# GpSimd takes over the splitting of queries and keys for four head pairs, and ScalarE scales one left-over probability tile

## The chip, the cores and the metric

The kernel runs on one core of one Trainium2 chip. The metric is the time of one execution on the device in microseconds; lower is better. The kernel before was timed three times.

## The reference, cut to what matters

Three stages follow each other, all in fp32, for 4 batches of 576 tokens with 8 heads of 64 (512 columns):

```python
# 1 attention with a threshold under the row's maximum
scores = scale * q @ k.T
scores = where(scores >= max(scores) - tau, scores, -1e9)
attn = exp(scores - max) / (sum + 1e-9)
x = attn @ v
# 2 a mixture over the sequence, then a channel MLP (512 -> 2048 -> 512)
u = x + (x.T @ U @ V).T
x = u + relu(u @ w_ch1) @ w_ch2
# 3 one of eight experts per token (512 -> 1024 -> 512), chosen by a gate
out = p[e] * (relu(x @ w1[e]) @ w2[e])
```

## The kernel before, in words

**Precision.** Most products are made from a high and a low part: the high part is the operand rounded to fp32r, the low part is the operand less the high part. For keys the scores multiply the queries with `kh` and with `kl`. For queries the 128 rows of `qs` hold the 64 rows of high parts above the 64 rows of low parts. Splitting a piece of raw data therefore takes a rounding copy and a subtraction.

**Pairs.** The heads are worked on two at a time, so a batch has four pairs; pair `i = 4 b + hp` belongs to batch `b`. `load_pair` (line 256 on) brings a pair in and splits it. Four pieces of a pair go through a ring of three buffers called `raw`: keys of 576 columns, keys of 640, queries of 608, queries of 608. In pairs 1 to 15, ScalarE makes the key's high part (L292) and the scaled query's rounded copy (L300), and VectorE makes the query's low half (L302). The key's low part (L293) is made by GpSimd in batches 0 and 1, and by VectorE later. In pair 0 two query pieces of 448 and 256 columns are already split by three GpSimd instructions each (L296 multiply in place, L297 rounding copy, L298 subtraction on 64 rows).

**Batch 0.** `attention_alone(0)` runs the attention of the first batch with no other matrix work beside it. A pair has five groups of rows, and nine score tiles of 128 rows by 576 keys: two tiles in groups 0 to 3 and one in group 4, which holds the left-over 64 rows of both heads. Per tile TensorE makes the scores (L321, L323), VectorE finds the row maximum (`peak`, L356) and the limits (L360), ScalarE the exponential (`exp`, L367) and VectorE the mask with the row sums (`mask`, L371). TensorE then transposes the masked tile (L427, and L433 to L438 for group 4), ScalarE moves it out of PSUM (L428, L434 to L440), and TensorE multiplies by V. Two score tiles fit in PSUM. The load of the next pair begins at its pair's third tile, one piece per tile.

**Normalization.** In batches 1 to 3 ScalarE multiplies every tile by the reciprocal row sums before the transposes (L381, in `norm`). In batch 0 the division is done late, in `chain`, once the product with V has been turned back into rows. For the left-over group that needs the second head's reciprocal on other partitions, which a small transfer on SP's queue brings there (L384), and two ScalarE instructions of 64 columns with two scales (L486).

**Beside batch 0.** `narrow` brings the 64-bit channel weights in as raw bits (`cr`, a ring of three), ScalarE casts one half (`top`, L212) and VectorE joins the halves (`w`, L219); the result is written to `wdram` and read back by `load_w` (`wr`), which splits it. In batch 0's channel weights ScalarE makes the high parts for `f` 0 and 1 (L692) and GpSimd for the other fourteen (L690); GpSimd makes the low parts (L693).

**Later.** From batch 1 on, `interleave` mixes the attention of one batch with the channel MLP of the batch before. The experts come last.

**Order.** A planner lays down each engine's order at compile time from its own estimates and the order of the program. GpSimd keeps the order of the program in batch 0's attention. Each engine, and SP's DMA queue too, then works strictly in the order laid down; a waiting instruction holds all that is behind it.

Of the kernel before, what the change touches and what calls it, by code (L numbers as in the profile page):

```python
# [14 lines left out]
AF = mybir.ActivationFunctionType  # L15
# [11 lines left out]
NPAIR = H // 2  # L27
# [76 lines left out]
def attention_channel_moe(ctx, tc, qk, vv, tau, umat, vrep, wch, wgl, wexp, consts, out):  # L104
# [156 lines left out]
    def load_pair(b, hp, later=None):  # L261

        i = b * NPAIR + hp
        v = ap.tile([128, VW], F32, tag="v", name=f"v{i}")
        qs = ap.tile([128, QKW], F32R, tag="qs", name=f"qs{i}")
        kh = ap.tile([128, QKW], F32R, tag="kh", name=f"kh{i}")
        kl = ap.tile([128, QKW], F32R, tag="kl", name=f"kl{i}")

        cuts = ((1, 0, S), (0, 0, 128), (1, S, QKW), (0, 704, 832), (0, 128, 256), (0, 832, 960),
                (0, 256, 704), (0, 960, QKW)) if i == 0 else (  # L270
            (1, 0, S), (1, S, QKW), (0, 0, 608), (0, 608, QKW))
        eng = dve if i == 0 or b > 1 else pool
        def steps():
            for n, (kq, c0, c1) in enumerate(cuts):
                c = slice(c0, c1)
                nm = f"raw{i}_{n}"
                if (i, n) == (0, 0):
                    x = mlp.tile([128, S], F32, tag="yr", name=nm, bufs=2)
                elif i == 0 and c1 - c0 == 128:
                    x = mlp.tile([128, 512], F32, tag="wr", name=nm, bufs=WR)  # L280
                else:
                    x = ap.tile([128, 640], F32, tag="raw", name=nm, bufs=3)
                x = x[:, :c1 - c0]
                sp.dma_start(out=x, in_=qk[i][:, kq, c])
                if (i, n) == (0, 1):
                    scalars()
                if (i, n) == (0, 5):
                    sp.dma_start(out=cst, in_=consts)
                if (i, n) == (0, 7):
                    sp.dma_start(out=wg_sb, in_=wgl)  # L290
                if kq:
                    act.activation(kh[:, c], x, AF.Copy)  # L292
                    eng.tensor_tensor(out=kl[:, c], in0=x, in1=kh[:, c].bitcast(F32), op=ALU.subtract)  # L293
                elif i == 0 and c1 - c0 > 128:
                    lo, hi, xl = qs[64:128, c], qs[64:128, c].bitcast(F32), x[64:128]
                    pool.tensor_scalar(out=x, in0=x, scalar1=t8[:, 1:2], scalar2=None, op0=ALU.mult)  # L296
                    pool.tensor_copy(qs[:, c], x)  # L297
                    pool.tensor_tensor(out=lo, in0=xl, in1=hi, op=ALU.subtract)  # L298
                else:
                    act.activation(qs[:, c], x, AF.Copy, scale=t8[:, 1:2])  # L300
                    lo, hi, xl = qs[64:128, c], qs[64:128, c].bitcast(F32), x[64:128]
                    dve.scalar_tensor_tensor(out=lo, in0=xl, scalar=t8[64:128, 1:2], in1=hi,  # L302
                                             op0=ALU.mult, op1=ALU.subtract)
                yield
            sp.dma_start(out=v, in_=vv[i])

        if later is None:
            for _ in steps():
                pass
        else:  # L310
            later.append(steps())
        return qs, kh, kl, v
# [13 lines left out]
    class Group:  # L326
# [47 lines left out]
        def norm(self):  # L374

            g = self.key[2]
            rv = self.rvs[:, g, 0:self.nh]
            if self.b >= SCALED:
                inverse(rv)
                for h in range(self.nh):  # L380
                    act.activation(self.pt[:, h], self.pt[:, h], AF.Copy, scale=rv[:, h:h + 1])  # L381
            elif g == 4:
                inverse(rv)
                sp.dma_start(out=self.rvs[:64, 4, 1:2], in_=self.rvs[64:, 4, 0:1])  # L384

    def inverse(x, on_act=False):
        if on_act:
# [70 lines left out]
    def chain(nm, hp, half, xT, xu, rvs):  # L458

        o, n = HALVES[half]  # L460
        if half == 0:
            if XS[0] is None:
                XS[0] = ap.tile([128, 5, 128], F32, tag="xsd", name=f"xsd{nm}", bufs=1)
                dve.memset(XS[0][64:, 4], 0.0)
        xsd = XS[0]
        c0, c1 = ((0, 2), (2, 5))[half]
        if rvs is not None:
            inverse(rvs[:, c0:c0 + 2], on_act=True)
        tp = po_tile(f"tx{nm}").rearrange("p (a b) -> p a b", a=4)
        for c in range(c0, c1):  # L470
            w = 64 if c == 4 else 128
            pe.transpose(tp[:w, c - c0], xu[:, c * 128 - o:c * 128 - o + w], ident)
        if rvs is None:
            dve.tensor_copy(xsd[:, c0:c0 + 2], tp[:, :2])
        else:
            dve.tensor_tensor(out=xsd[:, c0:c0 + 2].rearrange("p c (h d) -> p c h d", h=2),
                              in0=tp[:, :2].rearrange("p c (h d) -> p c h d", h=2),
                              in1=rvs[:, c0:c0 + 2].unsqueeze(3).to_broadcast([128, 2, 2, 64]), op=ALU.mult)
        if half == 0:
            yield 0.3  # L480
            return
        if rvs is None:
            act.activation(xsd[:64, 4], tp[:64, 2], AF.Copy)
        else:
            for h in range(2):
                act.activation(xsd[:64, 4, h * 64:h * 64 + 64], tp[:64, 2, h * 64:h * 64 + 64], AF.Copy,  # L486
                               scale=rvs[:64, 4, h:h + 1])
        yield 0.3
        while not MIXED[0]:
            next(conv)  # L490
        pst = po_tile(f"tT{nm}")[:, :128]

        for r, c in zip((0, 32, 64, 96), (4, 2, 3, 0)):
            pe.matmul(pst[r:r + 32], lhsT=u_sb[:, c], rhs=xsd[:, c], start=True, stop=False)
        for r in (0, 32, 64, 96):
            pe.matmul(pst[r:r + 32, r:r + 32], lhsT=u_sb[:, 1], rhs=xsd[:, 1, r:r + 32], start=False, stop=True)
        tT = ap.tile([128, 128], F32, tag="tT", name=f"tT{nm}", bufs=1)
        act.activation(tT, pst, AF.Copy)
        yield 0.7

        pr = po_tile(f"rep{nm}")[:, :128]
        pe.matmul(pr, lhsT=cst[:, C_REP:C_REP + 128], rhs=tT, start=True, stop=True)
        th = ap.tile([128, 128], F32R, tag="th", name=f"th{nm}", bufs=1)
        act.activation(th, pr, AF.Copy)
        dve.tensor_tensor(out=th[64:], in0=pr[64:], in1=th[64:].bitcast(F32), op=ALU.subtract)
        yield 0.3
        for (o, n), (c0, c1) in zip(HALVES, ((0, 2), (2, 5))):
            pu = po_tile(f"pu{nm}_{o}")
            u = xT[:, hp, o:o + n]
            if rvs is None:  # L510
                pe.matmul(pu[:, :n], lhsT=th, rhs=vst[:, o:o + n], start=True, stop=True)
                dve.tensor_tensor(out=u, in0=pu[:, :n], in1=u, op=ALU.add)
                yield 0.2
                continue
            for c in range(c0, c1):
                q = c * 128 - o
                pe.matmul(pu[:, q:q + 128], lhsT=xsd[:, c], rhs=ident, is_transpose=True, start=(c == c0), stop=False)
            pe.matmul(pu[:, :n], lhsT=th, rhs=vst[:, o:o + n], start=False, stop=True)
            act.activation(u, pu[:, :n], AF.Copy)  # L519
            yield 0.45  # L520
# [155 lines left out]
    def load_w(b, f):  # L676
        nm = f"{b}_{f}"
        if f >= NF or nm in W:
            return
        while DONE[0] < f:  # L680
            next(conv, None)
        r = []
        for i, bufs in ((0, W0), (1, W1)):
            x = mlp.tile([128, 512], F32, tag="wr", name=f"wr{nm}_{i}", bufs=WR)
            sp.dma_start(out=x, in_=wdram[f * 128:f * 128 + 128, i * 512:i * 512 + 512])
            hi = mlp.tile([128, 512], F32R, tag=f"w{i}h", name=f"w{i}h{nm}", bufs=bufs)
            lo = mlp.tile([128, 512], F32R, tag=f"w{i}l", name=f"w{i}l{nm}", bufs=bufs)
            eng = dve if b and (b < B - 1 or f < 8) else pool
            if b == 0 and f > 1:
                pool.tensor_copy(hi, x)  # L690
            else:
                act.activation(hi, x, AF.Copy)  # L692
            x = eng.tensor_tensor(out=lo, in0=x, in1=hi.bitcast(F32), op=ALU.subtract)  # L693
            if i == 0:
                LAST[:] = [x.ins]
            r.append((hi, lo))
        W[nm] = r
# [693 lines left out]
```

## Time and profile before

| | |
|---|---|
| time, median of 3 runs | 1032.04 us (1027.95 to 1032.97) |
| the profiled execution's own time | 1023.09 us |
| its span from first to last instruction | 1021.3 us |
| TensorE busy | 991.2 us (97%) |
| VectorE busy | 714.6 us (70%) |
| ScalarE busy | 612.4 us (60%) |
| GpSimd busy | 157.3 us (15%) |
| mean granted TensorE clock | 0.995 |

The busy times are sums over the whole span; the stages differ. TensorE's busy time counts matmuls that overlap in its pipeline.

### The profile page before, as it was taken

The page shows a single profiled execution, that of the slowest core. Times are in us where ns is not written, and L with a number is a line of the kernel's source. Part 1 is how long each engine was busy: PE and PEld are TensorE (multiplying, and loading weights), DVE is VectorE, ACT ScalarE, POOL GpSimd, SP SyncE. Part 2 cuts the span into 40 slices and gives each one's busy share as a digit, 9 for nine tenths or more (in the row PEclk, how much of TensorE's full clock was granted, in tenths as well). Part 3 has the DMA queues.
Part 4 walks back from the last instruction along what each step waited for, and adds up shares of the span by engine and source line. Part 5 has one row for each costly group of instructions (what it writes and reads, how often), then busy time and mean ns, then how long its engine had stood idle before and what let it go on. Part 6 is the DMA issues. An engine that isn't in the chain of part 4 may idle for free. (4 is left out here: it accounts for less than half of the span.)

```text
span 1021.3 us, 17791 instructions
## 1 busy us (share of the span) xinstructions
PE 991.2 (97%) x6308; PEld 830.7 (81%) x6309; DVE 714.6 (70%) x1764; ACT 612.4 (60%) x1250; POOL 157.3 (15%) x149
## 2 busy tenths in 40 slices
PE   8898999999999999999999999999999999999996
PEld 4666677778777787788888898999998898889884
DVE  7888686786778877777676564692369855566673
ACT  6898777776587776776575653422344444355562
POOL 3332246342000000000000000014400321020100
PEclk9999999999999999999999999999999999999998
DMA  6755487863322322322121110454054655566550
GB/s 212 240 149 174 155 271 229 282 206 127 125 93 95 115 87 71 125 98 87 56 69 42 42 44 30 140 201 137 27 199 167 209 175 186 174 197 202 187 185 17
DMA packets 58529, 143.72 MB, mean 141 GB/s; under 512 B 7421, under 2 KB 8573, under 8 KB 58432
## 3 DMA queue, kind: packets, MB, share of 16 engines
q1 hardware_dynamic: 55072, 132.27, 39.5%
q0 software_dynamic: 3360, 10.23, 3.1%
q8 instruction: 52, 0.85, 0.3%
q14 instruction: 45, 0.37, 0.1%
HBM read 124.65 MB, written 18.61 MB: 140 GB/s over the span
## 5 line engine op out<-in xcount | busy, mean ns | idle before, releaser
L1141 ACT ACTIVATE eh<-ew 128x512 fp32r<-128x512 f32 x160 | 94.2, 628 | 68.5 <-PE el L1257 54.0
L1142 DVE TENSOR_TENSOR el<-ew,eh 128x512 fp32r<-128x512 f32 x160 | 106.8, 692 | 38.6 <-ACT eh L1141 37.1
L714 PE MATMUL l<-uh,w0h 128*128 128x256 f32 (+2 forms) x352 | 126.8, 361 | 0.3 <-ACT yT L519 0.3
L371 DVE SCALAR_TENSOR_TENSOR p<-s,st,p 128x576 f32<-128x576 f32 x144 | 114.1, 815 | 18.3 <-ACT p L367 14.6
L367 ACT ACTIVATE p<-s,st 128x576 f32<-128x576 f32 x144 | 103.5, 738 | 34.2 <-DVE st L356 33.0
L715 PE MATMUL l<-ul,w0h 128*128 128x256 f32 (+2 forms) x352 | 122.6, 348 | 0.0
L716 PE MATMUL l<-uh,w0l 128*128 128x256 f32 (+2 forms) x352 | 122.3, 348 | 0.0
L356 DVE TENSOR_REDUCE st<-s 128x1 f32<-128x576 f32 x144 | 105.3, 750 | 16.4 <-PE s L323 15.4
L729 PE MATMUL l<-hh,w1h 128*128 128x512 f32 (+3 forms) x320 | 115.3, 360 | 0.0
L731 PE MATMUL l<-hh,w1l 128*128 128x512 f32 (+3 forms) x320 | 112.6, 352 | 0.0
L730 PE MATMUL l<-hl,w1h 128*128 128x512 f32 (+3 forms) x320 | 112.2, 351 | 0.0
L428 ACT ACTIVATE ptt<-tp 128x512 f32<-128x512 f32 (+1 forms) x192 | 88.5, 489 | 29.5 <-PE tp L427 29.2
L693 POOL TENSOR_TENSOR w1l<-wr,w1h 128x512 fp32r<-128x512 f32 x24 | 31.9, 1337 | 453.8 <-DVE rha L999 426.1
L321 PE MATMUL s<-kh,qs 128*128 128x288 f32 x320 | 95.8, 319 | 5.0 <-DVE p L371 2.7
L427 PE MATMUL tp<-cst,p 128*128 128x128 f32 x576 | 91.6, 276 | 3.9 <-ACT ptt L428 3.6
L734 DVE TENSOR_TENSOR yT<-l,yT 128x448 f32<-128x448 f32 (+2 forms) x96 | 50.0, 521 | 57.7 <-PE l L731 57.2
L323 PE MATMUL s<-kl,qs 128*128 128x288 f32 x320 | 88.9, 297 | 0.0
L381 ACT ACTIVATE p<-p,rv 128x576 f32<-128x576 f32 x108 | 78.6, 771 | 16.6 <-DVE rv L391 16.6
L427 PEld LDWEIGHTS tp<-cst,p 128*128 128x128 f32 x576 | 68.0, 140 | 20.2 <-ACT ptt L428 9.8
L447 PE MATMUL po<-ptt,v 128*64 128x256 f32 (+1 forms) x256 | 70.8, 414 | 1.6 <-ACT ptt L428 1.6
L321 PEld LDWEIGHTS s<-kh,qs 128*128 128x128 f32 x320 | 60.5, 189 | 14.4 <-DVE p L371 4.9
L446 PE MATMUL po<-ptt,v 128*64 128x256 f32 (+1 forms) x256 | 70.2, 413 | 1.7 <-ACT ptt L435 1.0
(612 smaller groups left out, 2436.4 us busy)
## 6 DMA issues: line engine op xcount, KB each, us to landing
ew<-in_wexp_dram SPq DMA_DIRECT2D x80, 512.0 KB, 4.6
wr<-wdram SPq DMA_DIRECT2D x128, 256.0 KB, 3.0
cr<-in_wch_dram SPq DMA_DIRECT2D x32, 512.0 KB, 5.2
raw<-in_qk_dram SPq DMA_DIRECT2D x30, 304.0 KB, 3.1
wdram<-w SPq DMA_DIRECT2D x32, 256.0 KB, 3.2
v<-in_vv_dram SPq DMA_DIRECT2D x16, 352.0 KB, 3.6
raw<-in_qk_dram SPq DMA_DIRECT2D x16, 320.0 KB, 3.5
raw<-in_qk_dram SPq DMA_DIRECT2D x16, 288.0 KB, 3.3
```

The lines of the kernel that those rows point to most:

```text
L321: pe.matmul(s["t"][:, h, :288], lhsT=qs[:, qc:qc + 128], rhs=kh[:, k0:k0 + 288], start=(j == 0), stop=False)
L356: dve.tensor_reduce(out=self.st[:, 0, h:h + 1], in_=self.t[h], axis=AX.XY, op=ALU.max, negate=True)
L367: act.activation(self.halves(h), self.t[h], AF.Exp, bias=self.st[:, 0, h:h + 1])
L371: dve.scalar_tensor_tensor(out=p, in0=self.t[h], scalar=self.st[:, 1, h:h + 1], in1=p, op0=ALU.is_ge, op1=ALU.mult, accum_out=self.rvs[:, ...
L427: pe.transpose(tp[:, c - c0], src[:, c * 128:c * 128 + 128], ident)
L714: pe.matmul(pm, lhsT=w1h[:, wk], rhs=uh[k], start=(k == 0), stop=False)
L715: pe.matmul(pm, lhsT=w1h[:, wk], rhs=ul[k], start=False, stop=False)
L716: pe.matmul(pm, lhsT=w1l[:, wk], rhs=uh[k], start=False, stop=(k == 3))
L729: pe.matmul(pm, lhsT=w2h[:, wd], rhs=xh, start=(f == f0), stop=False)
L730: pe.matmul(pm, lhsT=w2h[:, wd], rhs=xl, start=False, stop=False)
L731: pe.matmul(pm, lhsT=w2l[:, wd], rhs=xh, start=False, stop=(f == f0 + 3))
L1142: dve.tensor_tensor(out=lo, in0=x, in1=hi.bitcast(F32), op=ALU.subtract)
```

## The change

Pairs 1 to 4 (`own`) are split by GpSimd alone: a rounding copy and a subtraction for keys, and the three instructions of L296 to L298 for queries. ScalarE's and VectorE's instructions for these pairs go. In batch 0, the left-over tile is multiplied by its reciprocal row sums on ScalarE before the transposes, in place of the transfer on SP's queue and of the two scaled evictions, which become one plain one. GpSimd makes the high parts of the first batch's channel weights for `f` 0 and 1 too.

```diff
         eng = dve if i == 0 or b > 1 else pool
+        own = 1 <= i <= NPAIR
...
                 if kq:
-                    act.activation(kh[:, c], x, AF.Copy)
+                    if own:
+                        pool.tensor_copy(kh[:, c], x)
+                    else:
+                        act.activation(kh[:, c], x, AF.Copy)
                     eng.tensor_tensor(out=kl[:, c], in0=x, in1=kh[:, c].bitcast(F32), op=ALU.subtract)
-                elif i == 0 and c1 - c0 > 128:
+                elif own or i == 0 and c1 - c0 > 128:
                     lo, hi, xl = qs[64:128, c], qs[64:128, c].bitcast(F32), x[64:128]
                     pool.tensor_scalar(out=x, in0=x, scalar1=t8[:, 1:2], scalar2=None, op0=ALU.mult)
                     pool.tensor_copy(qs[:, c], x)
...
             elif g == 4:
                 inverse(rv)
-                sp.dma_start(out=self.rvs[:64, 4, 1:2], in_=self.rvs[64:, 4, 0:1])
+                act.activation(self.pt[:, 0], self.pt[:, 0], AF.Copy, scale=rv[:, 0:1])
...
-        if rvs is None:
-            act.activation(xsd[:64, 4], tp[:64, 2], AF.Copy)
-        else:
-            for h in range(2):
-                act.activation(xsd[:64, 4, h * 64:h * 64 + 64], tp[:64, 2, h * 64:h * 64 + 64], AF.Copy,
-                               scale=rvs[:64, 4, h:h + 1])
+        act.activation(xsd[:64, 4], tp[:64, 2], AF.Copy)
...
-            if b == 0 and f > 1:
+            if b == 0:
                 pool.tensor_copy(hi, x)
```

## Rows read from the trace of the kernel before

**Rows 1.** Busy time by stretch: microseconds and (instructions), clock, DMA share, GB/s.

```profile
core 0: us, PE busy (x) PEld busy (x) DVE busy (x) ACT busy (x) POOL busy (x), PEclk, DMA share, GB/s
28.41:51.38 22.97, 19.22 (x140) 13.73 (x138) 20.34 (x49) 19.30 (x43) 7.69 (x8) 1.00 0.71 236
51.38:75.00 23.62, 22.20 (x161) 16.05 (x160) 20.96 (x53) 21.12 (x47) 7.73 (x7) 1.00 0.49 144
...
125.00:900.00 775.00, 769.36 (x4928) 656.64 (x4927) 538.40 (x1378) 451.62 (x906) 106.58 (x98) 1.00 0.40 131
```

**Rows 2.** Waits of VectorE from 25 to 100 us: total, times, longest.

```profile
DVE p L371 <- ACT p L367: 2.8, 6, 1.0
DVE st L356 <- PE s L323: 1.8, 5, 0.5
```

**Rows 3.** Groups by shape on ScalarE and VectorE, 0 to 104 us.

```profile
L300 ACT ACTIVATE qs<-raw,t 128x608 fp32r<-128x608 f32 x10 | 7.9, 805 | 1.7 <-DMA raw<-in_qk_dram 1.7
...
L292 ACT ACTIVATE kh<-raw 128x640 fp32r<-128x640 f32 x6 | 4.4, 729 | 1.5 <-DMA raw<-in_qk_dram 1.5
L292 ACT ACTIVATE kh<-raw 128x576 fp32r<-128x576 f32 x6 | 4.1, 681 | 3.1 <-DMA raw<-in_qk_dram 3.1
...
L486 ACT ACTIVATE xsd<-tx,rv 64x64 f32<-64x64 f32 x6 | 1.5, 300 | 0.0
...
L692 ACT ACTIVATE w0h<-wr 128x512 fp32r<-128x512 f32 x2 | 1.3, 631 | 0.3 <-DMA wr<-wdram 0.3
...
L302 DVE SCALAR_TENSOR_TENSOR qs<-raw,t,qs 64x608 fp32r<-64x608 f32 x10 | 8.6, 870 | 0.6 <-ACT qs L300 0.3
...
L219 DVE SCALAR_TENSOR_TENSOR w<-cr,top 128x512 int32<-128x512 int32 x7 | 6.2, 889 | 0.0
```

**Rows 4.** Groups by shape on GpSimd, 0 to 104 us.

```profile
L293 POOL TENSOR_TENSOR kl<-raw,kh 128x640 fp32r<-128x640 f32 x5 | 8.2, 1643 | 0.0
L293 POOL TENSOR_TENSOR kl<-raw,kh 128x576 fp32r<-128x576 f32 x5 | 7.5, 1495 | 6.3 <-ACT kh L292 6.1
...
L296 POOL TENSOR_SCALAR raw<-raw,t 128x448 f32<-128x448 f32 x1 | 1.4, 1410 | 8.4 <-DMA raw<-in_qk_dram 8.4
L298 POOL TENSOR_TENSOR qs<-raw,qs 64x448 fp32r<-64x448 f32 x1 | 1.1, 1142 | 0.1
...
L296 POOL TENSOR_SCALAR raw<-raw,t 128x256 f32<-128x256 f32 x1 | 0.9, 922 | 0.1
L298 POOL TENSOR_TENSOR qs<-raw,qs 64x256 fp32r<-64x256 f32 x1 | 0.7, 732 | 0.1
...
L297 POOL CAST qs<-raw 128x448 fp32r<-128x448 f32 x1 | 0.6, 557 | 0.1
```

**Rows 5.** Timeline of GpSimd and TensorE where pair 1 begins: start, duration.

```profile
16.18 2.92 POOL L293 TENSOR_TENSOR kl<-raw,kh 128x576 fp32r<-128x576 f32 x2
...
29.28 0.38 PE L321 MATMUL s<-kh,qs 128*128 128x288 f32 x1
```

**Rows 6.** Timeline of GpSimd and VectorE from 31 to 36 us.

```profile
31.73 3.35 POOL L293 TENSOR_TENSOR kl<-raw,kh 128x576 fp32r<-128x576 f32 x2
...
34.06 1.57 DVE L219 SCALAR_TENSOR_TENSOR w<-cr,top 128x512 int32<-128x512 int32 x1
```

**Rows 7.** Left-over and scaled tiles, all batches: L381's durations (ns), who waited for it.

```profile
L381 ACT ACTIVATE p<-p,rv x108: 751/767/816, 107.6 to 610.7; 128x576 f32<-128x576 f32 x108
...
  PEld tp L433: 1.6, 6
```

**Rows 8.** Timeline of SP's queue and ScalarE; `cr` landings; SP's waits, 10 to 110 us.

```profile
19.14 4.38 SPq L284 DMA_DIRECT2D raw<-in_qk_dram  x3
...
23.66 6.85 SPq L204 DMA_DIRECT2D cr<-in_wch_dram  x3
...
28.97 0.79 ACT L212 ACTIVATE top<-cr 128x512 f16<-128x512 bf16 x1
...
DMA to landing us min/median/max: 3.5/4.7/5.2
...
SPq L284 <- POOL kl L293: 20.3, 7, 8.6
```

## The prediction

> **What bounds the kernel now.** I read the busy times by stretch first, since the change touches only what happens before about 104 us and the first batch's weights. From 125 to 900 us TensorE is busy 769.36 of 775.00 us [rows 1]; nothing the change takes off ScalarE or VectorE there can show. In batch 0 the picture is another. While pair 1 is worked on (28.41 to 51.38 us) VectorE is busy 20.34 of 22.97 us and ScalarE 19.30; while pair 2 is (51.38 to 75.00) they are busy 20.96 and 21.12 of 23.62 [rows 1]. The reader is to see two engines that are each about 88% full and hand the same tile to each other: peak, exponential, mask. GpSimd is at a third, 7.7 us in either stretch. The view of waits says what the rest of VectorE's time is: from 25 to 100 us the mask waits 2.8 us for ScalarE's exponential, in six places, and the peak 1.8 us for TensorE's scores [rows 2]. So batch 0 is bound by VectorE and ScalarE in turn, and what is cut there comes off the end, because TensorE's later work is merely started sooner.
>
> **The split of a pair, taken off.** ScalarE loses two key copies of 0.681 and 0.729 us and two query copies of 0.805: 3.02 us per pair. VectorE loses two query subtractions of 0.870: 1.74 us per pair [rows 3]. All four pairs count in this stage, since pair 4 is loaded ahead of batch 1.
>
> **The split of a pair, put on GpSimd.** The key subtractions are there already, 1.50 and 1.64 us. The multiply took 1.410 us for 448 columns and 0.922 for 256, so 2.54 ns a column and 1.82 us for 608. The subtraction on 64 rows took 1.142 and 0.732, so 1.48 us for 608. The copy took 0.557 us for 448 columns; in proportion 0.72, 0.80 and 0.76 us for 576, 640 and 608 [rows 4]. Keys: 0.72 + 0.80 + 1.50 + 1.64 = 4.66 us. Queries: 2 x (1.82 + 0.76 + 1.48) = 8.12. A pair takes 12.8 us of GpSimd where it took 3.1. That is hidden as long as a pair is ready before its first tiles, about 23 us after those of the pair before. Four pairs add 39 us to a third-full engine over some 85 us, which leaves it near 80%.
>
> **Pair 1 is the tight one.** GpSimd is busy with pair 0 until 16.18 us [rows 5], so pair 1 is whole at 16.18 + 12.8 = 29.0 us. Its second tile, the first that needs the last query piece, starts at 29.28 [rows 5]. TensorE works in order, so if that piece is late the transposes behind it wait too, and then ScalarE's evictions. I therefore count no gain at all for pair 1: the 1.74 to 3.02 us freed there are held by this arrival. The bounds are 0 and 1.74 us. Pairs 2 to 4 have their load begun some seven tiles ahead, and are counted fully.
>
> **Sum for pairs 2 to 4.** VectorE is the fuller of the two in the first of the stretches and level in the second, so its part is the base: 3 x 1.74 = 5.2 us. To this comes idle time of VectorE that ScalarE causes. With some 3 us fewer in ScalarE's queue per pair, a copy no longer stands in front of an exponential, and I take all of the 2.8 us and half of the 1.8 us, which come from TensorE waiting for evictions: 3.7 us [rows 2]. The bounds of this term are 0 and 4.6.
>
> **Weights.** Four copies of 0.631 us leave ScalarE [rows 3]. Their time lies between score tiles, where VectorE is the other bound, and they are part of the idle time just counted, so I add nothing; the bounds are 0 and 2.5 us. On GpSimd they are some 0.64 us each by the copy's proportion, well ahead of the channel's first matmul.
>
> **The left-over tile.** Per pair ScalarE gains a pass over 576 columns, 0.767 us [rows 7], and two evictions of 0.300 [rows 3] become one: +0.47 us, 1.9 us over four pairs, which the freed ScalarE covers. But TensorE's transposes of that tile now wait for the scaling. Later batches do the same: there the left-over transposes waited for it 1.6 us in 6 cases, 0.27 us each [rows 7]. Four times that is 1.1 us lost; bounds 0 and 4 x 0.767 = 3.1. The transfer on SP's queue was hidden, so its going gives nothing.
>
> **The lock between GpSimd and VectorE.** The join of the weight halves, which has two inputs in SBUF, started at 34.06 us in the middle of GpSimd's two subtractions and took 1.57 us; GpSimd was done at 31.73 + 3.35 = 35.08, and the join ended 0.55 us later [rows 6]. The seven joins of the stage took 6.2 us [rows 3], so the other six had 0.78 us each and the one blocked join cost 0.8 us. With GpSimd's share 2.5 times as large I expect 2.0 us of this, 1.2 more than now. The bounds are 0 and a wait of one whole subtraction, 1.50 us, for each of seven: 10.5 us.
> The Trainium skill says why (SBUF — State Buffer, Who interferes with whom): GpSimd and VectorE share one pair of ports under an exclusive lock, and a VectorE instruction with two SBUF inputs is fully blocked while a GpSimd instruction that reads SBUF has it. The trace agrees in the one row cited; read as a rule that every such join finds the lock taken, it gives the upper bound.
>
> **The sum.** 5.2 + 3.7 - 1.2 - 1.1 = 6.6 us. The profiled execution goes from 1023.09 to about 1016.5 us. It stands 9 us under the median of the runs shown, and the stage lies before the long matmul stretch, so I carry the 6.6 us over as they are: 1032.04 - 6.6 = 1025.4, given as 1025.5 us. Faster by over 0.5% means under 1026.9, slower means over 1037.2; half a per cent is the spread of the three runs, and about what a measurement of this kernel can tell from no change.
>
> **Rivals.**
> *ScalarE was the real limit.* For it: it is the fuller one from 51 to 75 us [rows 1]. Then its savings count: 3 x 3.02 + 2.5 - 1.9 = 9.7 us, 1022.3. Against it: VectorE hardly waits for it.
> *The lock takes it back.* Every join waits a whole subtraction: 10.5 in place of 1.2 us, 6.6 - 9.3 = -2.7, 1034.7 us. Against it: only one of seven is seen blocked now.
> *Pair 1 comes late.* If GpSimd's instructions run 1.25 times as long beside VectorE (3.35 against 2.92 us for two is 1.15 times, [rows 5, 6]), pair 1 is whole at 32.2 us, 2.9 late: 1028.4.
> *SP's queue is held by the raw ring (the other side).* GpSimd frees a raw buffer later than ScalarE and VectorE did. Pair 2's three loads were issued by 23.5 us, and the first three weight pieces stand behind them at 23.66 [rows 8]. If the order stays, the third load now waits for pair 1's last piece until 29.0, the weights follow at 29.2 and land a median of 4.7 us later, at 33.9; ScalarE's cast, which came at 28.97, holds the exponentials behind it for 4.9 us: 1030.4. If that repeats for pairs 3 and 4 it is 14.7 us, and 1025.5 + 14.7 = 1040. It decides from the second place on, where 9.8 exceeds 6.6. For it: SP already waits for GpSimd's key subtractions 20.3 us in 7 places, longest 8.6 [rows 8]. Against it: these waits are all hidden now, later casts have their data some tiles ahead, and the planner can put the weights first.
>
> **How the numbers follow.** Forecast 0.40, own range 1022.5 to 1029, of which 0.27 lies under 1026.9 and 0.13 above. ScalarE the limit 0.17, all faster. Lock 0.09, pair 1 late 0.08, SP's queue in one place 0.12: all within half a per cent. SP's queue in several places 0.14: slower. So faster 0.44, same 0.42, slower 0.14. The range 1019 to 1034.5 leaves out the last case and some 0.05 at the edges.
>
> **What would show it.** Right: from 28 us to the first scores of batch 1 the stage is 6 to 7 us shorter, VectorE some 1.7 and ScalarE 2.5 us less busy per pair, the mask's waits for the exponential nearly gone, GpSimd near 80%, and the stretch of matmuls after 125 us as long as before. Pair 1's second tile would start near 29 us and name GpSimd as what it waited for. Wrong: a cast waiting for `cr` by several microseconds, a left-over transpose waiting over 1 us for its scaling, joins of over 1.5 us in most places, or scores of pairs 2 to 4 released by GpSimd. A time outside the range would most likely come from the order that the planner lays down anew on SP's queue and ScalarE.

## The result, and the profile after

The changed kernel takes 1039.04 us (median of 9 runs, 1036.06 to 1043.33) beside 1032.57 for the kernel before (9 runs): a ratio of 1.0076 [1.0055, 1.0096], slower. The prediction said 1025.5, range 1019.0 to 1034.5. The profiled execution after took 1037.11 us with a span of 1035.3; that of before (1023.09) lies 4.9 us under the fastest of the nine, so their difference of 14 us overstates the loss, and I compare stretch by stretch. In the rows of after, the code from the scores to the transposes stands four lines lower than in the rows of before: L325 and L327 are the scores, L371 is the exponential, L375 the mask, L360 the peak; L285 is the raw load, L388 the new scaling of the left-over tile.

Where the time went is seen from the starts of the pairs, which I take from TensorE's timeline (the first scores of each pair, then the first matmul of batch 0's channel stage, all in us).

| kernel | pair 0 | pair 1 | pair 2 | pair 3 | batch 1 | channel |
|---|---|---|---|---|---|---|
| before | 5.96 | 28.41 | 51.38 | 72.56 | 96.51 | 110.58 |
| after | 6.01 | 25.73 | 58.70 | 79.78 | 103.64 | 118.67 |

Pair 0 is 2.7 us shorter, pair 1 is 10.0 us longer, pairs 2 and 3 are as long as before, and from batch 1's first scores to the channel it is 1.0 us more. The busy times by stretch of after, cut at these starts (columns as in [rows 1]):

```profile
25.73:58.70 32.97, 23.58 (x152) 17.55 (x150) 19.29 (x51) 17.94 (x40) 21.50 (x21) 0.84 0.63 199
58.70:79.78 21.08, 19.62 (x147) 14.67 (x146) 16.86 (x44) 16.67 (x37) 16.39 (x14) 1.00 0.39 119
79.78:103.64 23.86, 22.59 (x169) 16.65 (x167) 19.64 (x52) 19.28 (x43) 13.10 (x12) 1.00 0.54 175
125.00:900.00 775.00, 765.00 (x4887) 650.15 (x4885) 536.88 (x1376) 452.20 (x906) 106.77 (x98) 1.00 0.40 131
```

The same cut of before, for pairs 2 and 3:

```profile
51.38:72.56 21.18, 19.76 (x145) 14.41 (x143) 18.92 (x48) 18.68 (x43) 5.81 (x5) 1.00 0.45 134
72.56:96.51 23.95, 22.01 (x172) 16.93 (x170) 21.45 (x53) 21.13 (x47) 7.62 (x6) 1.00 0.53 156
```

In these two stretches the work left VectorE (18.92 to 16.86 and 21.45 to 19.64) and ScalarE (18.68 to 16.67 and 21.13 to 19.28) by 1.8 to 2.1 us each (1.7 and 2.5 forecast), and the stretches stayed at 21.1 and 23.9. TensorE is busy 93 and 95% of them.

Pair 1's ten microseconds are one chain, read here in the timeline of after, queue and engines in the order in which each held the next (start, duration; in brackets the idle time before it and what ended it):

```profile
26.98 1.48 POOL L302 TENSOR_TENSOR qs<-raw,qs 64x608 fp32r<-64x608 f32 x1
...
19.83 8.98 SPq L285 DMA_DIRECT2D raw<-in_qk_dram  x3
28.86 8.31 SPq L204 DMA_DIRECT2D cr<-in_wch_dram  x3
...
33.81 0.78 ACT L212 ACTIVATE top<-cr 128x512 f16<-128x512 bf16 x1 [8.27 <-DMA cr<-in_wch_dram]
34.45 0.71 ACT L371 ACTIVATE p<-s,st 128x576 f32<-128x576 f32 x1
35.06 0.37 ACT L457 ACTIVATE yT<-po 128x256 f32<-128x256 f32 x1
...
35.20 0.82 DVE L375 SCALAR_TENSOR_TENSOR p<-s,st,p 128x576 f32<-128x576 f32 x1 [7.63 <-ACT p L371]
...
35.49 0.69 PE L476 MATMUL tx<-cst,yT 128*128 128x128 f32 x2 [7.00 <-ACT yT L457]
...
36.26 0.59 PE L325 MATMUL s<-kh,qs 128*128 128x288 f32 x1
36.65 0.44 PE L327 MATMUL s<-kl,qs 128*128 128x288 f32 x1
...
39.49 0.29 PE L327 MATMUL s<-kl,qs 128*128 128x288 f32 x1
```

GpSimd is done with pair 1's last piece at 28.46. The third raw load of pair 2 needs that buffer, so SP's queue stands until then, and the first channel weights go out behind it at 28.86. ScalarE had come to their cast at 25.54 and waits 8.27 us. The exponential and an eviction stand behind the cast, and so the mask waits 7.63 us and TensorE 7.00. TensorE, VectorE and ScalarE are idle together. What follows costs more: the same score matmul then takes 0.44 us, where it takes 0.29 a little later. The same view by short stretches shows why:

```profile
28.00:34.00 6.00, 0.49 (x5) 0.25 (x3) 0.00 (x0) 0.19 (x1) 2.97 (x3) 0.86 0.69 214
34.00:38.00 4.00, 2.51 (x10) 2.17 (x11) 2.60 (x7) 3.88 (x8) 0.38 (x2) 0.50 0.15 30
38.00:42.00 4.00, 2.16 (x14) 1.90 (x12) 2.86 (x9) 3.04 (x6) 3.78 (x5) 0.85 0.90 286
42.00:46.00 4.00, 3.66 (x16) 2.92 (x18) 2.34 (x7) 2.67 (x7) 3.85 (x4) 0.57 0.88 253
46.00:50.00 4.00, 4.00 (x26) 2.34 (x23) 2.43 (x6) 1.38 (x4) 3.75 (x4) 1.00 0.62 211
```

The granted clock is 0.50 from 34 to 38 us, after TensorE stood for seven microseconds, and 0.57 from 42 to 46; before, the whole stretch had 1.00 [rows 1]. 0.50 is the lower of its two levels, 1.2 GHz.

### The profile page after: what moved, and what is told of

Same layout as the page of the kernel before. It is cut to its first block, busy times and chain, and to the rows that moved or that the text cites. A ratio compares the mean times of both kernels' runs of the same rounds, so it can differ in the third digit from the quotient of the medians.

```text
span 1035.3 us, 17801 instructions
## 1 busy us (share of the span) xinstructions
PE 996.3 (96%) x6308; PEld 834.2 (81%) x6309; DVE 710.3 (69%) x1756; ACT 603.3 (58%) x1230; POOL 197.8 (19%) x185
## 5 line engine op out<-in xcount | busy, mean ns | idle before, releaser
L375 DVE SCALAR_TENSOR_TENSOR p<-s,st,p 128x576 f32<-128x576 f32 x144 | 114.3, 815 | 27.9 <-ACT p L371 24.3
L371 ACT ACTIVATE p<-s,st 128x576 f32<-128x576 f32 x144 | 103.7, 738 | 38.9 <-DVE st L360 37.7
L360 DVE TENSOR_REDUCE st<-s 128x1 f32<-128x576 f32 x144 | 105.5, 751 | 21.9 <-PE s L327 21.3
L325 PE MATMUL s<-kh,qs 128*128 128x288 f32 x320 | 98.0, 326 | 4.2 <-DVE p L375 2.1
L327 PE MATMUL s<-kl,qs 128*128 128x288 f32 x320 | 89.8, 299 | 0.0
L325 PEld LDWEIGHTS s<-kh,qs 128*128 128x128 f32 x320 | 61.3, 192 | 15.2 <-issue 4.6
L713 PEld LDWEIGHTS l<-uh,w0h 128*128 128x128 f32 x352 | 66.4, 189 | 7.2 <-ACT yT L518 0.8
L450 PE MATMUL po<-ptt,v 128*64 128x256 f32 (+1 forms) x256 | 70.9, 415 | 1.1 <-ACT ptt L438 0.8
```

What stands on the lines that cost most here:

```text
L325: pe.matmul(s["t"][:, h, :288], lhsT=qs[:, qc:qc + 128], rhs=kh[:, k0:k0 + 288], start=(j == 0), stop=False)
L360: dve.tensor_reduce(out=self.st[:, 0, h:h + 1], in_=self.t[h], axis=AX.XY, op=ALU.max, negate=True)
L371: act.activation(self.halves(h), self.t[h], AF.Exp, bias=self.st[:, 0, h:h + 1])
L375: dve.scalar_tensor_tensor(out=p, in0=self.t[h], scalar=self.st[:, 1, h:h + 1], in1=p, op0=ALU.is_ge, op1=ALU.mult, accum_out=self.rvs[:, ...
L713: pe.matmul(pm, lhsT=w1h[:, wk], rhs=uh[k], start=(k == 0), stop=False)
```

## The experiments

Each ratio is to the kernel before on the same chip, with its interval. "Before" or "after" says which kernel was edited. The kernel before, run again as a control, had its pairs at 6.14, 29.38, 51.80, 72.98 and 97.09 and its channel start at 111.62. A start moves by up to a microsecond between executions, and a stretch by up to 0.8 us, more than the 0.5 that was expected.

> The kernel before, unchanged, for the scatter of one profile against another: the pair stretches (22.5, 23.0, 21.2, 23.9 us) and the first channel matmul (110.6 us) should come again within 0.5 us. If they scatter by 2 us or more, differences of that size between single profiles say nothing.

**The hold on SP's queue.** e1 and e2 take it away in two ways; e5 leaves it and takes away what stands around it.

e1, after, with pair 1 split as before:

```diff
-        own = 1 <= i <= NPAIR
+        own = 2 <= i <= NPAIR
```

> The changed kernel with pair 1 given back to ScalarE and VectorE; pairs 2 to 4 stay on GpSimd. Theory Q (the loss is SP's queue: three raw loads waiting for GpSimd's slow splits of pair 1 stand ahead of the first weight pieces, and ScalarE's cast waits for these): the cast's 8.3 us wait is under 1 us, TensorE's clock does not fall between 25 and 50 us, and the first channel matmul comes at 105 to 111 us against 118.67 in the changed kernel and 110.58 before; time 1026 to 1033. Rival G (GpSimd beside VectorE, or the scaled left-over tile, slows batch 0 as such): the first channel matmul stays at 115 or later, time 1036 or more.

e2, after, with pair 2's loads but the first queued behind the channel weights:

```diff
...
-                sp.dma_start(out=x, in_=qk[i][:, kq, c])
+                with tc.issue_after(CRS[4]) if i == 2 and n else nullcontext():
+                    sp.dma_start(out=x, in_=qk[i][:, kq, c])
```

> The changed kernel, with one thing more: on SP's queue the second and third raw load of pair 2 are issued behind the first two weight pieces instead of ahead of them. No work moves between engines. Theory Q: the 8.3 us wait of the cast falls under 2 us, the first channel matmul comes at 105 to 112 us, time 1026 to 1033. Rival G: nothing changes but a few hundred ns, time 1036 or more. Rival P (pair 1's late arrival from GpSimd is the loss): the scores of pair 1's second tile wait for GpSimd and the stage stays long.

e5, before, with only the split of the four pairs moved, neither the scaling nor the weights' copies:

```diff
+        own = 1 <= i <= NPAIR
...
+                    if own:
+                        pool.tensor_copy(kh[:, c], x)
...
+                elif own or i == 0 and c1 - c0 > 128:
```

> The kernel before with the splitting of pairs 1 to 4 on GpSimd alone, neither the scaling nor the weights' high parts. Theory Q: the cast waits about 8 us as in the changed kernel, first channel matmul at 115 to 119 us, time 1036 to 1041. Rival G by the scaling: time as before, 1032.

| kernel | time | ratio | pairs 1, 2, 3, batch 1, channel start at |
|---|---|---|---|
| e1 | 1029.86 | 1.0032 [1.0018, 1.0047] | 29.16, 51.07, 73.02, 96.83, 114.47 |
| e2 | 1028.80 | 1.0029 [1.0017, 1.0040] | 25.38, 53.14, 74.22, 98.09, 111.33 |
| e5 | 1043.77 | 1.0181 [1.0153, 1.0208] | 25.82, 56.39, 90.47, 114.65, 128.33 |

The kernel before takes 1025.85 us on the chip of these three, so the ratios count and not the times that were expected. Of the expected channel starts, e2's came; e1's and e5's came later than expected, and the reasons follow.

SP's timeline of e2, where the weights now go out first and the raw loads take the wait:

```profile
20.93 3.93 SPq L204 DMA_DIRECT2D cr<-in_wch_dram  x2
24.91 3.95 SPq L286 DMA_DIRECT2D raw<-in_qk_dram  x2
```

ScalarE's waits of e5 from 20 to 90 us (total, times, longest):

```profile
ACT w1h L696 <- DMA wr<-wdram: 11.2, 2, 10.4
ACT top L212 <- DMA cr<-in_wch_dram: 7.9, 1, 7.9
```

With this hold gone, by either way, the ratio falls from 1.0076 to 1.003: it cost about 4.6 us, 0.0045 of 1030. In e5 the same thing happens twice. SP's timeline there:

```profile
59.35 7.87 SPq L285 DMA_DIRECT2D raw<-in_qk_dram  x3
```

Pair 3's raw loads hold SP's queue from 59.35 to 67.22, the weights read back (`wr`) come late, and ScalarE, which makes their high parts in this kernel, waits 10.4 us for them. Pair 2's stretch is 34.1 us instead of 21.2. So the weights' part of the change has a use that I hadn't seen: it puts this second wait on GpSimd.

It isn't free there. GpSimd works in order too, and in e1 the split of pair 5's keys stands behind the waiting copy of a weight's high part (start, duration, idle time before and what ended it):

```profile
99.69 0.61 POOL L689 CAST w1h<-wr 128x512 fp32r<-128x512 f32 x1 [8.02 <-DMA wr<-wdram]
...
101.61 3.28 POOL L297 TENSOR_TENSOR kl<-raw,kh 128x576 fp32r<-128x576 f32 x2
...
104.92 0.33 SPq L285 DMA_DIRECT2D raw<-in_qk_dram  x1
...
106.39 0.80 ACT L304 ACTIVATE qs<-raw,t 128x608 fp32r<-128x608 f32 x1 [3.32 <-DMA raw<-in_qk_dram]
...
108.33 0.55 PE L476 MATMUL tx<-cst,yT 128*128 128x128 f32 x3 [3.80 <-ACT yT L457]
```

The raw load that needs the buffer goes out at 104.92, ScalarE waits 3.32 us for it with an exponential and an eviction behind, TensorE waits 3.80 us, and its granted clock is then 0.50 from 109 to 112 us. This is the same kind of hold once more. It accounts for e1's late channel start: its pairs stand as before, and only the stretch from batch 1's first scores to the channel is longer, 17.6 us where before has 14.1. After has it in small (GpSimd waits 7.7 us, ScalarE 1.0, TensorE 1.5). No run takes this second hold away, so its price is read from one profile.

In e2 the cast waits 1.9 us and no raw load holds ScalarE later; at the channel's first matmul it has lost nothing (111.33, the control 111.62). Yet it isn't faster. By its profile its 3 us come later: from there to the first scores of batch 2 it takes 169.2 us, the control 165.9 and before 164.0. What makes them isn't shown.

**The scaling of the left-over tile.** e3 is the kernel before with that part of the change alone; e8 is e1 without it, and e9 is e2 without it (the transfer and the two scaled evictions of before are back):

```diff
-                act.activation(self.pt[:, 0], self.pt[:, 0], AF.Copy, scale=rv[:, 0:1])
+                sp.dma_start(out=self.rvs[:64, 4, 1:2], in_=self.rvs[64:, 4, 0:1])
...
```

> The kernel before with the scaling of the left-over tile alone. Theory Q: no wait of several microseconds anywhere, the left-over transposes some 0.3 us later in each of four pairs, first channel matmul at 109 to 113 us, time within 0.3% of before. Rival G (the scaling is the loss): first channel matmul at 115 or later, time above 1036.

> The changed kernel with pair 1 split as before and without the scaling of the left-over tile: pairs 2 to 4 and the weights' high parts on GpSimd remain. If the scaling costs about 0.5% by itself, as it did on the kernel before, this is 0.4 to 0.6% faster than the kernel with pair 1 given back and the scaling in, so at or just under the time before: ratio 0.996 to 1.000. If the scaling costs only beside the old division, the ratio stays at 1.003.

> The changed kernel with the two weight pieces ahead of pair 2's raw loads on SP's queue, and without the scaling of the left-over tile: all four pairs and the weights' high parts stay on GpSimd. Theory Q with a price of its own for the scaling: pair 0's stretch 19.5 us, no wait of the cast above 2 us, no left-over transpose waiting 2 us for a scaling, first channel matmul at 106 to 109 us, ratio 0.994 to 0.999. If GpSimd beside VectorE were the loss, the ratio would stay at 1.003 or more.

e3 took 1031.14 us, ratio 1.0052 [1.0032, 1.0072]; e8 1029.48, 1.0030 [1.0008, 1.0051], where e1 has 1.0032; e9 1030.90, 1.0040 [1.0023, 1.0057], where e2 has 1.0029. Alone the scaling costs half a per cent; taken out of the change it gives nothing back. A cost that depends so much on its surroundings isn't that of an instruction; in e3's profile pair 1 takes 25.6 us and TensorE's granted clock is 0.50 from 34 to 40 us. e3 and e9 missed what was expected, e8 came out at the second of its two cases. By its expectation e9's 1.0040 would speak for GpSimd slowing VectorE, but VectorE's instructions aren't slower in after: from 51 to 103 us a mask takes 0.815 us (before 0.814) and a row maximum 0.754 (before 0.755).

**What a microsecond is worth on each engine.** Three kernels add work to the kernel before, in batch 0 or its pairs 1 to 4. x1 runs each low-part score matmul of batch 0 twice (the low part then counts double), x2 each of ScalarE's splitting copies twice, x3 each query subtraction of VectorE a second time into a spare place:

```diff
+                for again in range(2 if s["b"] == 0 else 1):
+                    pe.matmul(s["t"][:, h, :288], lhsT=qs[:, qc:qc + 128], rhs=kl[:, k0:k0 + 288],
...
+                    for again in range(2 if 1 <= i <= NPAIR else 1):
+                        act.activation(kh[:, c], x, AF.Copy)
...
+                        dve.scalar_tensor_tensor(out=spare, in0=xl, scalar=t8[64:128, 1:2], in1=hi,
+                                                 op0=ALU.mult, op1=ALU.subtract)
```

> The kernel before with every score matmul of the keys' low parts in batch 0 issued twice (the low part then counts double): 80 matmuls of about 0.13 us more on TensorE, 2.6 us per pair. Theory T (TensorE's stream binds the stretches of pairs 2 and 3, 21.2 and 23.9 us): they grow by 1.8 to 2.8 us each. Theory A (VectorE and ScalarE bind): by under 0.7 us each.

> The kernel before with ScalarE's key and query copies of pairs 1 to 4 each issued twice: 3.0 us more on ScalarE per pair, the same values. Theory A: the stretches of pairs 1 to 3 grow by 2 to 3 us each. Theory T: under 1 us each. If all engines bind in turn, growth is seen here and with the doubled matmuls alike.

> The kernel before with VectorE's query subtraction of pairs 1 to 4 issued a second time into the spent raw buffer: 1.74 us more on VectorE per pair, the same values. Theory A: the stretches of pairs 1 to 3 grow by 1.2 to 1.7 us each. Theory T: under 0.6 us each.

| kernel | ratio | pairs 1, 2, 3, batch 1, channel start at |
|---|---|---|
| x1 | 1.0060 [1.0024, 1.0097] | 29.54, 55.28, 79.19, 105.22, 119.17 |
| x2 | 1.0035 [1.0017, 1.0052] | 28.84, 55.08, 76.70, 98.98, 115.12 |
| x3 | 1.0056 [1.0028, 1.0084] | 30.37, 53.86, 77.54, 104.11, 118.66 |

Batch 1 starts 8.7 us later for the 10 us more of TensorE (x1), 7.6 us later for the 7 us more of VectorE (x3), and 2.5 us later for the 12 us more of ScalarE (x2; its channel start is 4.5 us later). By pairs, x1 makes pairs 1 to 3 longer by 2.8, 2.7 and 2.1 us, as theory T had it; x3 by 0.5, 2.5 and 2.6; x2 makes pair 1 longer by 3.3, pair 2 by 0.4 and pair 3 shorter by 1.7. In pairs 2 and 3 TensorE and VectorE bind together and ScalarE has slack. The order of the work was laid down anew in these kernels too, which (below) can be worth several microseconds, so only the small numbers for ScalarE in these two pairs against those near the full amount are a safe reading.

Four more take work away. e7, before, has no low-part score matmuls in batch 0; x5 has the same on e2. e6, before, has pairs 1 to 4 brought in by casting transfers, with neither split nor scaling of the queries; it routes tokens otherwise, and only its first 260 us can be read. x6, before, moves pair 1 alone to GpSimd, with the weights first.

> The kernel before without the score matmuls with the keys' low parts in batch 0: 80 matmuls of about 0.13 us less on TensorE, 2.6 us per pair, and nothing else left out. Theory T: the stretches of pairs 2 and 3 get shorter by 1.5 to 2.6 us each. Theory A: by under 0.6 us each, and VectorE and ScalarE are as full as before.

> The changed kernel with the weight pieces first and, in batch 0, without the score matmuls of the keys' low parts: ScalarE, VectorE and TensorE are all relieved, by some 3.0, 1.7 and 2.6 us per pair. Theory B (TensorE and VectorE bind together): the stretches of pairs 2 and 3 (21.1 and 23.9 us with the splitting moved alone) fall by 1.5 us or more each wherever the granted clock stays at 1. If a chain of latencies from score to mask binds instead, they fall by under 0.7 us.

> The kernel before, with pairs 1 to 4 brought by GpSimd's casting transfers straight into the tiles of the high and the low parts: neither the scaling of the queries nor the split is computed for these pairs, on any engine, and no raw buffer is used. Theory A (the forecast's: VectorE and ScalarE bind pairs 2 and 3): their stretches, 21.2 and 23.9 us before from first score to first score, fall to about 19.2 and 22.0 us, and the first channel matmul comes some 6 us before 110.6. Theory T (TensorE's stream, worked in order, binds them): both stretches stay within 0.7 us of before, so that a split that costs nothing is worth under 2 us there; only pair 0's stretch gets shorter, by about 3 us.

> The kernel before with pair 1 alone split on GpSimd and the two weight pieces ahead of pair 2's raw loads. If pair 0's stretch is the one where freed time counts, it takes 19.5 us in place of 22.5, nothing else changes, and the first channel matmul comes 2 to 3 us earlier: ratio 0.996 to 0.999. If the 3 us are given back in pair 1's stretch, as in every run so far, the ratio is 1.000 or more.

| kernel | ratio | pairs 1, 2, 3, batch 1 start at |
|---|---|---|
| e7 | 1.0014 [1.0000, 1.0029] | 27.33, 53.96, 76.19, 98.73 |
| x5 | 1.0032 [1.0013, 1.0051] | 26.73, 51.65, 75.56, 96.53 |
| e6 | 1.0521 [1.0500, 1.0543], not to be read | 25.80, 54.70, 74.16, 98.58 |
| x6 | 1.0051 [1.0033, 1.0068] | 25.80, 55.84, 76.98, 102.17 |

None gains, in time or at the start of batch 1. This was a puzzle: more work is slower and less work is slower too. Yet single stretches do get shorter. x5 relieves all three engines; its busy times in pairs 2 and 3:

```profile
51.65:75.56 23.91, 20.69 (x134) 13.97 (x133) 18.32 (x48) 17.42 (x38) 19.69 (x17) 0.93 0.37 118
75.56:96.53 20.97, 19.09 (x142) 13.64 (x141) 18.95 (x49) 17.94 (x41) 12.77 (x12) 1.00 0.59 182
```

Where the granted clock stays at 1.00, in pair 3, it takes 3.0 us less than before (23.95), as theory B had it. e7's pair 3 (22.54) is 1.4 us shorter, and e6's pair 2 (19.46), with no splitting on any engine, 1.7 us shorter, as theory A had it; its pair 3 is not. What is won is lost elsewhere. e6's pair 1 takes 28.9 us, where ScalarE waits 3.6 us for the weights read back and TensorE 3.6 us behind it. x5 and e7 lose in the stretches with a lower clock; e7's busy times show it:

```profile
28.00:52.00 24.00, 19.58 (x127) 13.97 (x126) 20.47 (x51) 18.96 (x43) 8.46 (x8) 0.93 0.76 227
52.00:74.00 22.00, 17.48 (x103) 12.24 (x102) 17.68 (x46) 17.56 (x40) 5.20 (x4) 0.84 0.47 140
```

TensorE has fewer matmuls to do, stands more, and is then granted 0.93 and 0.84. From 25 to 125 us the mean granted clock is 1.00 in before, x0, x1 and, of the runs below, e4 and p1, and 0.90 to 0.98 in every other profile. Another part is the order.

**The order in which TensorE's work is laid down.** e4, before, moves nothing but the four copies of the weights' high parts:

```diff
-            if b == 0 and f > 1:
+            if b == 0:
```

> The kernel before with the high parts of the first batch's weights for f 0 and 1 on GpSimd alone: four copies of 0.63 us off ScalarE. With TensorE and VectorE binding, no gain: the first channel matmul within 1.5 us of 110.6, ratio 0.998 to 1.002.

It took 1028.73 us, ratio 1.0031 [1.0014, 1.0048], though it takes work off ScalarE and puts it on GpSimd, the emptiest engine. But with 2.5 us fewer on ScalarE the planner lays down another order on TensorE in batch 0: pair 2's scores, for one, come ahead of transposes that they stood behind. Three kernels hold that order. TensorE's 5829 matmuls and transposes of the main program are the same in all of them; each is queued behind the one that precedes it in a given kernel, with an edge that orders and doesn't wait:

```diff
...
+    for x, y in zip(rows, rows[1:]):
+        tc.add_manual_dep(y, x.name, mybir.DependencyInfo(
+            mybir.DependencyClass.NoSync, mybir.DependencyReason.DATA), reason="row")
...
```

p1 is e4 in the order of before, p3 is e2 in the order of before, p4 is the kernel before in the order of e2.

> The weights' part of the change alone (four copies of the early channel weights' high parts on GpSimd instead of ScalarE, nothing else), with TensorE's matmuls and transposes held in the order in which the kernel before issues them. Alone and with TensorE's order left free it ran at a ratio of 1.0031 [1.0014, 1.0048], with VectorE's row maxima waiting 6.3 us for scores in the first batch (2.6 before). Theory O (the loss comes from the other order that TensorE's work is laid down in as soon as durations elsewhere change): a ratio of 0.998 to 1.001, and that wait back below 3.5 us. Rival W (the loss comes from the moved work itself, in GpSimd's and VectorE's rows): 1.002 to 1.005 as without the held order.

> The whole change with the channel weights' transfers issued ahead of the third raw load (ratio 1.0029 [1.0017, 1.0040] with TensorE's order left free), here with TensorE held in the order of the kernel before. Theory O: 1.000 or faster, down to the 0.9935 that the prediction's 6.6 us for pairs 2 to 4 would give. Rival W: 1.002 to 1.005, the stretch of pair 1 again some 5 us longer than before. A third case: TensorE bound in all of these stretches whatever the order, 0.998 to 1.002 with pairs 2 and 3 unchanged at 21.1 and 23.9 us.

> The kernel before, with all its work where it was, but TensorE held in the order in which the change with its transfers issued earlier lays TensorE's work down. Theory O: slower by what that kernel is slower, a ratio of 1.002 to 1.006, with VectorE's row maxima waiting 4 to 10 us for scores. Rival W: 0.999 to 1.001.

| kernel | time | ratio | with its own order |
|---|---|---|---|
| p1 | 1025.41 | 0.9996 [0.9981, 1.0011] | 1.0031 [1.0014, 1.0048] |
| p3 | 1034.77 | 1.0092 [1.0066, 1.0119] | 1.0029 [1.0017, 1.0040] |
| p4 | 1038.35 | 1.0125 [1.0100, 1.0149] | 1 |

VectorE's waits from 6 to 97 us, of e4:

```profile
DVE st L356 <- PE s L323: 6.3, 11, 1.4
```

of p1:

```profile
DVE st L356 <- PE s L323: 3.6, 8, 0.8
```

and of p4:

```profile
DVE st L356 <- PE s L323: 7.3, 10, 3.0
DVE p L371 <- ACT p L367: 6.5, 8, 1.7
```

For the smallest edit this settles it: the same work on the same engines is 0.35% faster in the old order, and the peaks' wait for scores falls from 6.3 to 3.6 us (the expectation said below 3.5; before has 2.6, the control 4.2). p4 shows what an order alone can do: no work moved, and 1.25% lost, more than the whole change lost. For the change itself, though, my expectation fell. In the order of before it is slower still, 1.0092, so the new order alone isn't what stands between the change and its gain. p3's stretches of pairs 1 to 3 say more:

```profile
28.79:54.19 25.40, 20.22 (x141) 14.39 (x139) 19.07 (x51) 16.77 (x37) 19.61 (x18) 0.93 0.71 234
54.19:76.00 21.81, 19.69 (x145) 14.70 (x143) 17.19 (x46) 16.85 (x37) 16.58 (x14) 1.00 0.39 115
76.00:99.04 23.04, 22.20 (x171) 16.93 (x170) 19.82 (x52) 19.15 (x43) 12.43 (x11) 1.00 0.58 182
```

TensorE does the same rows in the same order as before. In pairs 2 and 3 VectorE has 3.4 us less to do (17.19 + 19.82 beside 18.92 + 21.45) and ScalarE 3.8, and the two stretches together take 44.85 us where they took 45.13 (45.29 in the control): 0.3 us, no more than the scatter. p3 loses around them: in pair 1, with a clock of 0.93, and from batch 1's first scores (99.04) to the channel (118.26), 19.2 us at a clock of 0.85 where before has 14.1 at 1.00. GpSimd waits 8.9 us for the weights there, as in e1, and ScalarE 1.1 us for a raw load; the rest of these 5 us isn't traced.

## Why the prediction was wrong

Right were the durations. GpSimd finished pair 1 at 28.46 where I had 29.0. The groups on GpSimd and VectorE in the first 112 us of after, by shape:

```profile
L300 POOL TENSOR_SCALAR raw<-raw,t 128x608 f32<-128x608 f32 x8 | 14.8, 1845 | 3.6 <-DMA raw<-in_qk_dram 3.2
L302 POOL TENSOR_TENSOR qs<-raw,qs 64x608 fp32r<-64x608 f32 x8 | 12.2, 1525 | 0.7
L297 POOL TENSOR_TENSOR kl<-raw,kh 128x640 fp32r<-128x640 f32 x5 | 8.1, 1617 | 0.2
L297 POOL TENSOR_TENSOR kl<-raw,kh 128x576 fp32r<-128x576 f32 x5 | 7.6, 1527 | 0.2
L301 POOL CAST qs<-raw 128x608 fp32r<-128x608 f32 x8 | 5.5, 689 | 0.4
...
L219 DVE SCALAR_TENSOR_TENSOR w<-cr,top 128x512 int32<-128x512 int32 x7 | 5.3, 755 | 0.0
```

1.85, 1.53 and 0.69 us stand against 1.82, 1.48 and 0.76 forecast. That the later work would only shift also held, against the control: from the channel's first matmul to the end of the span after takes 916.6 us and x0 915.7 (before's own profile 910.7).

Of the signs that I had listed, the cast waiting for `cr` by several microseconds and the left-over transposes waiting over 1 us are there, both on the list for wrong. Point by point:

*"So batch 0 is bound by VectorE and ScalarE in turn, and what is cut there comes off the end."* This is the step that failed first, and with it the terms 5.2 and 3.7 us for pairs 2 to 4. TensorE stood in the same rows with 19.22 of 22.97 and 22.20 of 23.62 us [rows 1]: 84% in the first, less than VectorE, but 94% in the second, fuller than either engine that I named. (The second row also runs 2.4 us into pair 3; cut at 72.56, TensorE has 93% and VectorE 89.) The added work of x1 to x3 says that TensorE and VectorE bind pairs 2 and 3 together, x5's pair 3 that relief on all three engines is worth 3.0 us, and p3, with TensorE's work and order as before, that 3.4 us less on VectorE and 3.8 on ScalarE are worth 0.3. (e6's pair 2, 1.7 us shorter with no split at all, is the one stretch that speaks for my step.) The idle time of VectorE didn't vanish. The waits of VectorE while pairs 2 and 3 are worked on, in before (51.38 to 96.51) and in after (58.70 to 103.64):

```profile
DVE st L356 <- PE s L323: 1.5, 4, 0.5
DVE p L371 <- ACT p L367: 0.8, 2, 0.6
...
DVE st L360 <- PE s L327: 4.4, 7, 1.0
DVE p L375 <- ACT p L371: 3.0, 4, 1.4
```

That is 7.4 us where before has 2.3. The wait for the exponential, which I had as going, grew as well: VectorE, with less to do, waits longer.

*SP's queue held by the raw ring.* The rival was right in its place and its chain, and its landing (33.9 forecast, 33.81 seen); I gave it 0.26 in all. Its price was mis-sized. I kept the cast at 28.97, where it came before [rows 8], and got 4.9 us; but ScalarE, freed of pair 1's copies, was there at 25.54, so the same landing cost 8.27. The clock wasn't in the sum at all: from 34 to 46 us TensorE was granted 0.50, 0.85 and 0.57. Repeating for pairs 3 and 4, which I had as the slower case, wasn't needed for a slower kernel, because there was no 6.6 us to set against it. A second hold did come, at pair 5's load, over a path that I hadn't: GpSimd's own wait for the weights (1.0 us on ScalarE in after, 3.3 in e1).

*Pair 1 counted at nothing.* Its split was done in pair 0's stretch, which became 2.7 us shorter. That time was given back at once: in e2, with no hold, pair 1 takes 27.8 us where it took 23.0. e9, which has no scaling either, takes 23.6 us for pair 1, keeps 0.6 us at pair 2's start (50.79) and loses it in pair 2 (23.8 us, at a clock of 0.93).

*The weights* were counted at nothing for their 2.5 us off ScalarE, and p1 agrees: with TensorE's order held, 0.9996 [0.9981, 1.0011]. But I had them on GpSimd "well ahead of the channel's first matmul" and asked only who waits for them, not what GpSimd would wait for: it stands 7.7 us for the weights in after and 8.0 in e1, with pair 5's split behind.

*The left-over tile.* Forecast 1.1 us of waiting, measured once, 2.2 us (the transposes for the scaling, in pair 1), and none in the other three pairs. In e2 it is 2.2 us again, behind 1.9 us for a mask, and the granted clock is 0.52 from 34 to 41 us. Its own 0.77 us lay on ScalarE, which had room.

*The lock between GpSimd and VectorE.* Forecast 1.2 us lost; the joins fell from 0.889 us [rows 3] to 0.755. I had read too little of before: two of its seven joins were blocked, at 34.06 (1.57 us) and at 94.41 (1.26), and the five others took 0.68, so the lock cost 1.5 us and not 0.8. In after three joins meet an idle GpSimd (0.68), two start inside its multiply (0.68 and 0.69), and two inside a rounding copy (0.73 and 1.14). One of each:

```profile
77.01 1.80 POOL L300 TENSOR_SCALAR raw<-raw,t 128x608 f32<-128x608 f32 x1 [3.24 <-DMA raw<-in_qk_dram]
78.00 0.68 DVE L219 SCALAR_TENSOR_TENSOR w<-cr,top 128x512 int32<-128x512 int32 x1
...
88.47 0.69 POOL L301 CAST qs<-raw 128x608 fp32r<-128x608 f32 x1
88.57 1.14 DVE L219 SCALAR_TENSOR_TENSOR w<-cr,top 128x512 int32<-128x512 int32 x1
```

The second ends 0.55 us behind the copy, as the join at 34.06 in before did behind the subtraction. The lock cost 0.5 us in after, so 1 us came back. The Trainium skill (SBUF — State Buffer, Who interferes with whom) has a join with two SBUF inputs wait while a GpSimd instruction that reads SBUF holds the ports. The two joins beside copies agree; the two inside the multiply, which reads SBUF as well, do not. The upper bound of 10.5 us was far off.

In numbers: forecast -6.6 us, measured +7.8 (0.0076 of 1032.57; interval 5.7 to 9.9). Of these 14 us the hold with its half clock is about 4.6, shown by e1 and e2. The 6.6 that I had for pairs 2 to 4 aren't there, by the unchanged stretches of after and by p3. The rest, 3 us or 0.3%, is what e1 and e2 still lose. For e1 the profile shows a second hold of that size; for e2, which loses behind the channel's start, the cause stays open. That an order alone can cost as much is shown by p1 and p4; that it is the cause here isn't, since giving e2 the order of before made it worse. An order in which the freed time comes off the end may exist; none was found, and no kernel here beat the kernel before.

## What to carry to other kernels

Read every engine's row of the stretch before you name what binds it, and count a saving only if TensorE, or whichever is fullest, has idle time there that the saved work ended. Before moving the release of a ring's buffers to a slower engine, list what stands behind the ring's loads on the same DMA queue and what that engine itself will wait for in between, and take the time at which the reader will arrive after the change, not before it. Where a planner lays the order down from durations, an edit anywhere near can cost 0.3% by the new order alone (e4 beside p1; an order laid down for another kernel cost 1.25% in p4); hold the order fixed in an experiment before a small loss is put down to the work.

## What the runs showed of the hardware

TensorE's clock multiplied a stall: after it had stood for 7.0 us the granted clock was 0.50 from 34 to 38 us, and after a further 2.2 us of standing 0.57 from 42 to 46, with score matmuls at 0.44 us where the same ones take 0.29 at 39.49; from 46 to 50 it was 1.00 again. Less work had the same effect (e7: 0.93 and 0.84). GpSimd, at 78% in pair 2's stretch where it had been at 27% (5.81 of 21.18), did its key subtractions in 1.53 and 1.62 us beside 1.50 and 1.64 [rows 4]. What a VectorE instruction with two inputs in SBUF lost by it hung on what GpSimd was doing: a join of 0.68 us that started inside a copy or a subtraction ended 0.55 us behind it (1.14 us in after, 1.57 and 1.26 in before), while two in after and two in e2 that started inside a multiply kept 0.68 or 0.69 us. One in e9 that started inside a multiply took 1.02.
